# Diagonal sums by VectorE from scaled tiles in the later half of a fused linear-attention and MLP kernel, with a new order table

## The chip, the cores and the metric

The kernel runs on one core of one Trainium2 chip. The metric is device time in microseconds (us) of one execution, from launch to end; lower is better. The profile of one execution gives a span, from the first to the last recorded instruction, which is a little shorter than that execution's device time.

In the profile PE is TensorE's matrix multiply, PEld its weight load, DVE is VectorE, ACT is ScalarE, POOL is GpSimd and SP is SyncE, which here only starts transfers. A q behind an engine's name is its instruction queue.

## The reference

A linear attention with a decaying state feeds an MLP (all inputs float32, output 3072 x 384 float32):

```python
B, H, S, D = 4, 8, 768, 48
for t in range(S):
    cur = einsum('bhd,bhe->bhde', u * k[:, :, t], v[:, :, t])
    y[:, :, t] = einsum('bhd,bhde->bhe', r[:, :, t], state + cur)
    state = w * state + einsum('bhd,bhe->bhde', k[:, :, t], v[:, :, t])
x = y.transpose(0, 2, 1, 3).reshape(B * S, H * D)          # 3072 x 384
h = maximum(x @ w_in, 0)                                    # d_ff = 2048
out = (h * h) @ w_out
```

The term with `u` is the diagonal: at time t it adds `v[t] * sum_d(r[t,d] * u[d] * k[t,d])` for each head. These sums over d, eight per row (one per head), are what the change moves.

## The kernel before

The 768 time steps of each of the 4 batches are cut into 6 chunks of 128. A unit is one chunk of one batch: unit i has chunk i // 4 and batch i % 4, so there are 24. Units 0 to 5 are handled singly; units 6 to 23 in pairs (i, i + 1), where loads, transposes and some elementwise steps take both units at once, and the first matrix product of the MLP takes both as 256 columns.

Steps of a unit, by the names that the order table uses:

- `rt`, `kt`, `vt`: loads of r, k and v. SP's queue issues r and k (units 0 to 5 in two halves each, `rt.1.0` and `rt.1.1`), POOL's queue issues v of units 0 to 5; later v comes by SP too (`vtS` and `vt`). `ktA` is a load from ACT's queue.
- `scale.i.0` and `scale.i.1` (VectorE, L301 and L303): r times a rising and k times a falling power of w, into the bf16 tile `rkw`, 48 values of a head padded to 64.
- `turn`, `rkT` (TensorE, ScalarE; units 0 to 5) or `rkD` (one transposing DMA for a pair): `rkT`, r and k with head dimension on the partitions.
- `rk` (VectorE, L357 for pairs, L360 for single units): product of the transposed r and k, 128 x 1024 in bf16 for a pair.
- `at` (TensorE, L369): scores of a unit or pair; `mask` (VectorE, L377), two per unit: scores times the triangle.
- `d` or the first part of `s`: the diagonal sums, four products with `rk` as weights and `uwb` (u times w on a block diagonal) as 8 moving columns, L389 or L410. The second part of `s`, L398, is the state's update, left out for the last chunk. `sadd`, `sdec` (VectorE, L424, L428) and `stb` (ScalarE, L432) carry the state on.
- `dv` (VectorE, L420): v times the diagonal sums. `y` (TensorE, L441, L447): masked scores times v plus r times state. `yb` (VectorE, L456): their sum, bf16.
- `xturn`, `xT` or `xD` (a transposing DMA for a pair, L467): y transposed. `m1.i.s` (TensorE, L493): x times a quarter or an eighth of `w_in`; for a single unit, `m1.i.s` uses the weights `w_in_q` number s. `relu` (ScalarE, L501), `sqA` or `sqD` (square by ScalarE, L508, or by VectorE, L510). `m2` (TensorE, L517, and L533 for the last unit): times `w_out`. `osb` and `out`: the result's copy and its store.
- `I.q` and `O.q`: POOL's loads of the weights `w_in_q` and `w_out_q` number q. `ids`, `upper`, `zeros`, `copied`, `uwb`: small constants. `fill.n`: n products of a constant tile that give TensorE something to do.

The order table ORDER is a list of these words. The kernel walks it once and issues the instructions of each step as it meets the word; each engine and each queue then runs its own instructions in that order, and the number behind @ names the PSUM bank. A wait therefore holds everything that stands later on the same engine. The schedule is entirely this table. `by_rows`, `rows_of` and the like do not exist before.

Of the kernel before, what the change touches and what calls it, by code (L numbers as in the profile page):

```python
# [16 lines left out]
kt.0.0 kt.0.1 rt.0.0 rt.1.0 I.0 rt.1.1 vt.0 ktA.1.0 lnat.0 fill.26 log@4567 kt.1.1 lnat.1 ids rt.2.0 w.1 upper w.0  # L17
fill.8 cols@1 rt.2.1 wk scale.0.0 kt.2.0 zeros scale.0.1 wr fill.8 turn.0.0@2 kt.2.1 copied uwb turn.0.1@5 rkT.0.0
rt.3.0 rkT.0.1 vt.1 rk.0 fill.10 at.0@63 scale.1.0 rt.3.1 I.3 kb.0@4 mask.0.0 d.0@2 turn.1.0@7 I.2 kbT.0 kt.3.0
mask.0.1 rkT.1.0 vt.2 scale.1.1 vb.0 I.1 kt.3.1 fill.19 turn.1.1@4 dv.0 y.0@3 rkT.1.1 rt.4.0 yb.0 vb.1 rk.1 fill.9  # L20
kb.1@4 kt.4.0 scale.2.0 at.1@31 xturn.0@6 rt.4.1 mask.1.1 d.1@5 turn.2.0@2 xT.0 rkT.2.0 scale.2.1 kt.4.1 fill.5
m1.0.0@7 kbT.1 mask.1.0 turn.2.1@2 relu.0.0 dv.1 rt.5.0 fill.2 y.1@1 rkT.2.1 m1.0.3@4 yb.1 end rt.5.1 s.1@5
scale.3.0 relu.0.3 wend xturn.1@7 rk.2 at.2@26 xT.1 kb.2@0 mask.2.1 sqA.0.0 kt.5.0 d.2@4 turn.3.0@3 vt.3 s.0@7
sadd.1 rkT.3.0 m1.0.2@1 kt.5.1 scale.3.1 kbT.2 O.0 m1.1.0@6 mask.2.0 vb.2 relu.0.2 vt.4 turn.3.1@3 dv.2 m1.1.3@5
rt.6 rkT.3.1 sadd.0 O.1 y.2@1 relu.1.0 kt.6 m1.1.2@0 yb.2 relu.1.3 vt.5 at.3@72 rk.3 relu.1.2 kb.3@4 mask.3.1
xturn.2@6 sqA.1.0 O.2 m1.0.1@5 scale.4.0 xT.2 s.2@0 O.3 sqD.0.3 d.3@2 relu.0.1 m1.1.1@1 vb.3 mask.3.0 turn.4.0@3
kbT.3 m1.2.0@6 scale.4.1 relu.1.1 dv.3 m1.2.1@4 rkT.4.0 sqD.1.3 sqA.0.2 y.3@7 m1.2.2@1 scale.5.0 relu.2.1 sqD.1.1
m1.2.3@2 relu.2.2 sqD.0.1 s.3@5 sqA.1.2 turn.4.1@4 m2.0.0@3 sadd.3 relu.2.3 sadd.2 m2.1.0@1 rkT.4.1 yb.3 relu.2.0
m2.1.1 rk.4 vb.4 scale.5.1 kb.4@7 stb.1 xturn.3@6 at.4@42 kbT.4 m2.0.1 mask.4.1 xT.3 stb.0 s.4@5 mask.4.0 turn.5.0@6
m1.3.0@2 sqD.2.1 rkT.5.0 y.4@0 dv.4 relu.3.0 turn.5.1@6 rt.8 sadd.4 m1.3.3@7 rkT.5.1 yb.4 m2.1.2 sqA.3.0 sqA.2.0  # L30
m2.0.2 kt.8 xturn.4@2 m2.0.3 xT.4 scale.6.0 kb.5@5 osb.0 m2.1.3 scale.7.0 relu.3.3 m1.3.1@2 vtS.6 kbT.5 vb.5
m1.4.0@6 scale.6.1 scale.7.1 at.5@75 relu.4.0 m2.2.0@0 mask.5.0 osb.1 rkD.6 sqA.4.0 m1.4.1@4 sqD.2.3 sqA.2.2 sqD.3.3
m1.4.2@1 relu.3.1 mask.5.1 m2.2.1 stb.3 sdec.4 m1.4.3@6 relu.4.2 rt.10 rk.5 y.5@5 sqA.4.2 scale.8.0 s.5@2 scale.8.1
relu.4.1 m2.2.2 scale.9.0 relu.4.3 vtS.8 m1.3.2@1 sqD.3.1 stb.4 m2.3.0@4 dv.5 relu.3.2 yb.5 m2.2.3 scale.9.1 kt.10
m2.3.1 osb.2 sadd.5 sqA.4.1 m2.4.0@1 sqD.4.3 vb.6 xturn.5@0 sdec.5 at.6@2376 xT.5 rk.6 rkD.8 m2.4.1 stb.2 mask.7.0
stb.5 m1.5.0@0 sqA.3.2 mask.6.0 s.7@7 relu.5.0 mask.7.1 m1.5.3@5 mask.6.1 s.6@2 relu.5.3 m2.4.2 dv.6 out.0 vb.8
y.6@3 dv.7 rt.12 y.7@0 yb.6 m1.5.1@6 yb.7 m2.3.2 sadd.6 relu.5.1 xD.6 scale.10.0 m2.4.3 sqA.5.0 scale.10.1 sqA.5.1
m2.3.3 sadd.7 vtS.10 osb.4 m1.5.2@6 scale.11.1 scale.11.0 m2.5.0@3 relu.5.2 sqD.5.3 kt.12 m2.5.1 sqA.5.2 rk.8
at.8@1520 osb.3 sdec.6 m2.5.2 mask.9.0 rkD.10 m2.5.3 mask.8.0 s.8@4 mask.8.1 osb.5 s.9@2 m1.6.0@7 mask.9.1 m1.6.1@6
sadd.8 relu.6.0 dv.9 kt.14 m1.6.3@5 relu.6.1 dv.8 m1.6.7@1 sqA.6.0 scale.12.0 sadd.9 sqA.6.1 y.9@3 rt.14 y.8@4 vb.10  # L40
m1.6.2@0 yb.8 stb.6 m1.6.5@2 yb.9 relu.6.3 sdec.9 xD.8 m1.6.4@6 relu.6.5 scale.12.1 m2.7.0@3 relu.6.2 sqD.6.3
relu.6.7 vtS.12 m2.6.0@4 scale.13.0 relu.6.4 scale.13.1 m1.6.6@7 sqA.6.2 rk.10 at.10@6120 sqA.6.4 rkD.12 m2.6.1
relu.6.6 mask.10.0 sqA.6.5 s.10@5 sdec.7 m2.7.1 sqA.6.6 sqD.6.7 m2.7.2 stb.7 mask.10.1 stb.9 out.1 m2.7.3 sadd.10
kt.16 mask.11.0 y.10@6 osb.7 m1.8.0@1 dv.10 m1.8.1@2 rt.16 scale.14.0 relu.8.0 sdec.8 m1.8.3@5 relu.8.1 mask.11.1
m2.6.2 stb.8 yb.10 sqA.8.1 s.11@3 y.11@2 relu.8.3 dv.11 m1.8.6@1 vb.12 yb.11 m1.8.4@6 relu.8.6 sadd.11 xD.10 m2.6.3
rk.12 sqA.8.0 relu.8.4 scale.15.0 m1.8.2@2 scale.14.1 m1.8.5@0 relu.8.2 sdec.10 out.4 m2.9.0@7 osb.6 scale.15.1
vtS.14 sqA.8.2 sqD.8.3 m2.8.0@6 relu.8.5 out.3 at.12@4312 sqA.8.6 rkD.14 s.12@0 sqA.8.5 mask.13.0 m2.8.1 sqA.8.4
mask.12.1 m1.8.7@5 mask.12.0 m1.10.1@1 relu.8.7 mask.13.1 out.2 m1.10.3@3 relu.10.1 scale.16.0 vtS.16 s.13@4 sadd.12
# [35 lines left out]
def kernel(  # L84
# [130 lines left out]
    def fill():  # L215
        nc.tensor.matmul(out=banks[0][:, :128], lhsT=warm, rhs=warm, start=True, stop=True)  # L216
# [165 lines left out]
    def apart(i):  # L382
        return f" d.{i}@" in ORDER.replace("\n", " ")
# [239 lines left out]
```

## Time and profile before

| what | value |
|---|---|
| device time, median of 3 runs (lowest to highest) | 171.85 us (170.75 to 172.5) |
| device time of the profiled execution | 171.94 us |
| its span | 170.2 us |
| mean granted TensorE clock | 0.988 |
| DVE, ACT busy | 122.3 us, 129.8 us |

The profiled execution lies 0.09 us above the median of the runs, and 1.74 us of its device time lie outside the span. The busy time of PE is that of pipelined instructions, whose recorded durations overlap: how fast PE works is read from the distance between the starts of successive groups.

### The profile page before, as it was taken

The numbers are of one execution on the slowest core, as the hardware profiler recorded it, in microseconds if no ns is written. First come the engines' busy times: TensorE is split into PE (matmuls) and PEld (weight loads), VectorE is DVE, ScalarE is ACT, GpSimd is POOL, SyncE is SP. The second block draws the span as 40 slices with busy tenths as digits, with TensorE's granted clock in tenths as the row PEclk, the third lists the DMA queues.
The fourth block names the chain that finished last, engine by engine and source line by source line (L and its number), as shares of the span: only waits on it lengthen the run. The fifth ranks groups of instructions, "written<-read, shape, count | busy, mean of one in ns | idle before, by whom it ended". The sixth has DMA issues, their size and how long they took to land.

```text
span 170.2 us, 4733 instructions
## 1 busy us (share of the span) xinstructions
PE 163.9 (96%) x1947; PEld 134.1 (79%) x1947; DVE 122.3 (72%) x243; ACT 129.8 (76%) x255; POOL 15.7 (9%) x36
## 2 busy tenths in 40 slices
PE   7959999999999999999999999999999999999993
PEld 7649999778787697886977887787889789688672
DVE  6567999876999989988988888989697662101100
ACT  3735999888796489698499679688699739599921
POOL 7770670000000000000000000000000000000000
PEclk9996999999999999999999999999999999999999
DMA  3999999999999899999999997998990501100044
GB/s 92 172 279 240 272 194 254 213 201 227 185 181 218 153 214 190 181 212 191 236 182 202 174 251 173 188 288 197 180 232 4 179 6 54 42 0 4 0 164 162
DMA packets 91493, 28.86 MB, mean 170 GB/s; under 512 B 82864, under 2 KB 90672, under 8 KB 91472
## 3 DMA queue, kind: packets, MB, share of 16 engines
q1 hardware_dynamic: 88416, 23.99, 67.5%
q0 software_dynamic: 2624, 4.33, 12.9%
q8 instruction: 15, 0.25, 0.6%
q10 hardware_dynamic: 432, 0.25, 0.6%
q14 instruction: 6, 0.05, 0.1%
HBM read 20.50 MB, written 4.72 MB: 148 GB/s over the span
## 4 chain that ended last, share of the span: by engine, by line
PE 87%; DMA 6%; DVE 3%; SPq 2%; issue 1%; DVEq 0%
PE bank L493 36%; PE bank L517 34%; DMA rt<-in_r_dram 4%; PE bank L369 4%; PE bank L441 3%; DMA xT<-yb 2%; PE bank L398 2%; PE bank L447 2%; SPq L281 2%; PE bank L533 2%; PE bank L333 1%; PE bank L410 1%; PE bank L345 1%; PE bank L216 1%; PE bank L477 1%
## 5 line engine op out<-in xcount | busy, mean ns | idle before, releaser
L493 PE MATMUL bank<-xT,w_in_q 128*128 128x256 bf16 (+1 forms) x720 | 72.6, 251 | 0.1
L501 ACT ACTIVATE gr<-bank 128x512 f32<-128x512 f32 x96 | 55.3, 604 | 19.0 <-PE bank L493 15.2
L517 PE MATMUL bank<-w_out_q,g 128*128 128x384 bf16 x368 | 68.6, 326 | 0.0
L493 PEld LDWEIGHTS <-w_in_q 128*128 128x128 bf16 x720 | 63.8, 113 | 3.9 <-DMA xT<-yb 0.3
L517 PEld LDWEIGHTS <-g 128*128 128x128 bf16 x368 | 34.3, 98 | 18.1 <-issue 0.2
L508 ACT ACTIVATE g<-gr 128x512 bf16<-128x512 f32 x68 | 41.2, 636 | 0.2
L377 DVE TENSOR_TENSOR am<-bank,smask 128x512 bf16<-128x512 f32 x48 | 31.3, 684 | 7.4 <-PE bank L369 6.6
L510 DVE TENSOR_TENSOR g<-gr 128x512 bf16<-128x512 f32 x28 | 19.0, 686 | 17.2 <-ACT gr L501 17.2
L524 ACT COPY osb<-bank 128x384 f32<-128x384 f32 x23 | 11.0, 480 | 5.7 <-PE bank L517 5.6
L456 DVE TENSOR_TENSOR yb<-bank,dv 128x384 bf16<-128x384 f32 x24 | 12.9, 553 | 3.2 <-PE bank L447 2.3
L420 DVE TENSOR_TENSOR dv<-vb,bank 128x384 f32<-128x384 bf16 x24 | 13.0, 548 | 2.2 <-PE bank L410 1.4
L432 ACT CAST stb<-st 128x384 bf16<-128x384 f32 x20 | 10.2, 522 | 0.6 <-DVE st L428 0.6
L301 DVE TENSOR_TENSOR rkw<-rt,wpos 128x384 bf16<-128x384 f32 x18 | 9.8, 551 | 0.8 <-DMA rt<-in_r_dram 0.7
L301 DVE TENSOR_TENSOR rkw<-kt,wneg 128x384 bf16<-128x384 f32 x18 | 9.7, 551 | 0.8 <-DMA kt<-in_k_dram 0.8
L337 ACT COPY rkT<-bank 128x512 bf16<-128x512 bf16 x12 | 7.0, 590 | 3.4 <-PE bank L333 3.4
L216 PE MATMUL bank<-warm 128*128 128x128 bf16 x87 | 8.4, 265 | 1.1 <-DVE warm L161 1.1
L441 PE MATMUL bank<-vb,am 128*128 128x48 bf16 x192 | 8.9, 185 | 0.0
L428 DVE TENSOR_TENSOR st<-st,wend 128x384 f32<-128x384 f32 x16 | 8.8, 550 | 0.0
L424 DVE TENSOR_TENSOR st<-bank,st 128x384 f32<-128x384 f32 x16 | 8.7, 549 | 0.0
L441 PEld LDWEIGHTS <-am 128*128 128x128 bf16 x192 | 7.9, 97 | 0.8
L369 PE MATMUL bank<-rkT 64*128 64x128 bf16 x192 | 8.2, 221 | 0.2 <-ACT rkT L337 0.2
L216 PEld LDWEIGHTS <-warm 128*128 128x128 bf16 x87 | 7.0, 121 | 1.2 <-DVE warm L161 1.0
(75 smaller groups left out, 120.8 us busy)
## 6 DMA issues: line engine op xcount, KB each, us to landing
out_dram<-osb SPq DMA_DIRECT2D x23, 192.0 KB, 2.4
rt<-in_r_dram SPq DMA_DIRECT2D x9, 384.0 KB, 5.8
kt<-in_k_dram SPq DMA_DIRECT2D x9, 384.0 KB, 5.2
vt<-in_v_dram SPq DMA_DIRECT2D x9, 384.0 KB, 4.5
w_in_q<-in_moe_w_in_dram POOLq DMA_DIRECT2D x4, 384.0 KB, 8.3
w_out_q<-in_moe_w_out_dram POOLq DMA_DIRECT2D x4, 384.0 KB, 8.8
vt<-in_v_dram POOLq DMA_DIRECT2D x6, 192.0 KB, 7.3
kt<-in_k_dram SPq DMA_DIRECT2D x11, 96.0 KB, 5.2
```

The costliest lines, as they stand in the source:

```text
L216: nc.tensor.matmul(out=banks[0][:, :128], lhsT=warm, rhs=warm, start=True, stop=True)
L301: nc.vector.tensor_tensor(t["rkw"][:, x, :, :, :D], pair(src), pair(wneg if x else wpos), ALU.mult)
L369: nc.tensor.matmul(out=t["at"][o][:, p, :], lhsT=t["rkT"][sl, 1, p, :], rhs=t["rkT"][sl, 0, p, :], start=True, stop=True,)
L377: nc.vector.tensor_tensor(am, t["at"][o], smask.unsqueeze(1).to_broadcast([C, HP, C]), ALU.mult)
L420: nc.vector.tensor_tensor(t["dv"], t["vb"], t["d"].unsqueeze(2).to_broadcast([C, H, D]), ALU.mult)
L441: nc.tensor.matmul(out=y[:, 2 * p + o, :], lhsT=t[f"am{o}"][:, p, :], rhs=t["vb"][:, 2 * p + o, :], start=(o == 0 and p == 0), stop=c == 0 ...
L456: nc.vector.tensor_tensor(t["yb"], t["y"], t["dv"].rearrange("p h d -> p (h d)"), ALU.add)
L493: nc.tensor.matmul(out=t["h", s][:, a], lhsT=turned, rhs=chunks[c]["xT"][:, b : b + m, n, :], start=(n == 0), stop=(n == NK - 1),)
L501: nc.scalar.activation(t["gr", s], t["h", s], AF.Relu)
L508: nc.scalar.activation(g, x, AF.Square)
L510: nc.vector.tensor_tensor(g, x, x, ALU.mult)
L517: nc.tensor.matmul(out=t["o"], lhsT=chunks[units[i][0]]["g"][:, f, units[i][1], :], rhs=w_out_q[f // 4][:, f % 4, :], start=(f == 0), stop ...
```

## The change

For pairs 12 to 22 (units 12 to 23) the sums no longer go through the transposed tiles. VectorE makes three instructions of a pair instead of the one `rk`: `dx` multiplies the scaled r and k of both units (128 x 768, bf16 in and out, into the buffers of `rk`), `du` multiplies this by a row of u times w that lies on every partition (128 x 768, bf16 and float32 in, float32 out, into the tile of `dv`), and `dr` adds up the 48 values of each head (128 x 768 to 128 x 16). `dv` reads these sums from SBUF instead of PSUM. TensorE's four products with 8 columns go away for these 12 units; `s.20` to `s.23`, which held nothing else, go away altogether. Units 0 to 11 keep the old way.

The row of u times w needs two more loads on POOL's queue, `wB` and `uB` (each one row of 384 values to all 128 partitions, into buffers of `osb`), and one product on POOL, `uw`. The loads of w and u that the columns need (`wu`) and the logarithm `lnw` become words of the table. `dv` becomes a tile of a pair with 2 buffers. Four squares move from VectorE to ScalarE (28 to 24 `sqD`, 68 to 72 `sqA`); `rk` goes from 15 to 9. The table is another one from its first line on.

```diff
+    def spread_row(name):
+        rows[name] = mpool.tile([128, dm], F32, name="osb")
+        src = dict(uB=u, wB=w)[name].rearrange("h d -> (h d)")
+        nc.gpsimd.dma_start(out=rows[name], in_=src.unsqueeze(0).to_broadcast([128, dm]))
+
+    def uw_row():
+        nc.gpsimd.tensor_tensor(uw, rows["uB"], rows["wB"], ALU.mult)
...
+    def by_rows(i):
+        return i >= NH and f" dx.{i // 2 * 2} " in ORDER.replace("\n", " ")
+
+    def rows_of(i):
+        whole = two("rk", i, work, [128, HP, C], bufs=RKB)
+        return whole.rearrange("p u a c -> p u (a c)")[:, :, :dm]
+
+    def diag_product(i):
+        x = rkw_b[i // 2 % NPAD].rearrange("p u x a o e -> p u x (a o) e")[:, :, :, :, :D]
+        nc.vector.tensor_tensor(rows_of(i).rearrange("p u (h d) -> p u h d", h=H), x[:, :, 0], x[:, :, 1], ALU.mult)
+
+    def diag_weigh(i):
+        whole = of_two("dv", i, work, [C, H, D], F32, bufs=2)
+        nc.vector.tensor_tensor(
+            whole.rearrange("p u h d -> p u (h d)"), rows_of(i), uw.unsqueeze(1).to_broadcast([128, 2, dm]), ALU.mult
+        )
+
+    def diag_add(i):
+        whole = of_two("dd", i, work, [C, H], F32, bufs=3)
+        nc.vector.tensor_reduce(whole, two("dv", i, work, [C, H, D], F32, 2), axis=mybir.AxisListType.X, op=ALU.add)
...
     def sums(i):
         c, b = units[i]
         whole = bank("s", i)
-        if not apart(i):
+        if not apart(i) and not by_rows(i):
...
     def diag_v(i):
         t = tiles[i]
-        t["dv"] = work.tile([C, H, D], F32, name="dv")
-        nc.vector.tensor_tensor(t["dv"], t["vb"], t["d"].unsqueeze(2).to_broadcast([C, H, D]), ALU.mult)
+        of_two("dv", i, work, [C, H, D], F32, bufs=2)
+        d = t["dd"] if by_rows(i) else t["d"]
+        nc.vector.tensor_tensor(t["dv"], t["vb"], d.unsqueeze(2).to_broadcast([C, H, D]), ALU.mult)
...
-kt.0.0 kt.0.1 rt.0.0 rt.1.0 I.0 rt.1.1 vt.0 ktA.1.0 lnat.0 fill.26 log@4567 kt.1.1 lnat.1 ids rt.2.0 w.1 upper w.0
+wu kt.0.0 rt.0.0 kt.0.1 rt.1.0 wB lnw rt.1.1 vt.0 ktA.1.0 lnat.0 fill.26 log@4567 kt.1.1 lnat.1 w.0 ids rt.2.0 w.1
...
```

At the start of the program, POOL's instructions before, from its constants on (`vt` is v of unit 1, then of unit 2; `w_in_q0` was issued well ahead of this, just behind the loads of w and u):

```order
L226 MEMSET uwb_136 128x32
L227 MEMSET wend_146 128x384
L256 TENSOR_TENSOR cols_126<-cols_126 128x4
L259 CAST uwb_136<-cols_126 64x4 x2
L311 DMA vt_162<-in_v_dram 128x8x48
L288 DMA w_in_q3_150<-in_moe_w_in_dram 128x3x512
L288 DMA w_in_q2_149<-in_moe_w_in_dram 128x3x512
L311 DMA vt_310<-in_v_dram 128x8x48
L288 DMA w_in_q1_148<-in_moe_w_in_dram 128x3x512
```

The same place on POOL now:

```order
L302 DMA w_in_q0_142<-in_moe_w_in_dram 128x3x512
masks.py:65 MEMSET smask_130 128x128
masks.py:66 AFFINE_SELECT smask_130<-smask_130 128x128
L232 MEMSET uwb_131 128x32
L233 MEMSET wend_141 128x384
L262 TENSOR_TENSOR cols_121<-cols_121 128x4
L265 CAST uwb_131<-cols_121 64x4 x2
L325 DMA vt_232<-in_v_dram 128x8x48
L302 DMA w_in_q3_145<-in_moe_w_in_dram 128x3x512
L302 DMA w_in_q2_144<-in_moe_w_in_dram 128x3x512
L302 DMA w_in_q1_143<-in_moe_w_in_dram 128x3x512
```

`w_in_q0` has moved behind the loads of w's row and of v of units 0, 1 and 2, and between the product for `uwb` and `w_in_q3` stands the load of v of unit 3 instead of that of unit 1.

On VectorE, from the first scaling (of unit 0) on, before (`cols` is the copy that POOL's product for `uwb` waits for, L253):

```order
L303 TENSOR_TENSOR rkw0_127<-rt_88,wfour_123 128x8x48
L303 TENSOR_TENSOR rkw0_127<-kt_155,wfour_123 128x8x48
L253 COPY cols_126<-bank1_77 128x8
L360 TENSOR_TENSOR rk_267<-rkT_241 128x512
L303 TENSOR_TENSOR rkw0_127<-rt_88,wfour_123 128x8x48
L377 TENSOR_TENSOR am0_294<-bank6_257,smask_135 128x512
L377 TENSOR_TENSOR am1_307<-bank3_79,smask_135 128x512
L303 TENSOR_TENSOR rkw0_127<-kt_155,wfour_123 128x8x48
L420 TENSOR_TENSOR dv_340<-vb_313,bank2_78 128x384
L456 TENSOR_TENSOR yb_353<-bank3_79,dv_340 128x384
```

And now:

```order
L317 TENSOR_TENSOR rkw0_122<-rt_88,wfour_118 128x8x48
L317 TENSOR_TENSOR rkw0_122<-kt_154,wfour_118 128x8x48
L259 COPY cols_121<-bank6_252 128x8
L374 TENSOR_TENSOR rk_279<-rkT_227 128x512
L412 TENSOR_TENSOR am1_306<-bank6_252,smask_130 128x512
L412 TENSOR_TENSOR am0_309<-bank2_78,smask_130 128x512
L374 TENSOR_TENSOR rk_279<-rkT_227 128x512
L456 TENSOR_TENSOR dv_340<-vb_293,bank3_79 128x384
L317 TENSOR_TENSOR rkw1_123<-rt_208,wfour_118 128x8x48
L492 TENSOR_TENSOR yb_359<-bank7_253,dv_340 128x384
L412 TENSOR_TENSOR am0_376<-bank2_78,smask_130 128x512
```

Both scalings of unit 1 (the two rows at the top of this fence; unit 0's stand just ahead of them) now come ahead of the copy of the columns and of unit 0's masks.

In the later half, on VectorE around the masks of a pair, before (pair 14: `rk`, four masks, then `dv` and `yb` of both units, with the state and squares between):

```order
L357 TENSOR_TENSOR rk_1845<-rkT_1667 128x1024
L377 TENSOR_TENSOR am1_1852<-bank2_78,smask_135 128x512
L377 TENSOR_TENSOR am0_1860<-bank5_256,smask_135 128x512
L377 TENSOR_TENSOR am1_1872<-bank6_257,smask_135 128x512
L377 TENSOR_TENSOR am0_1875<-bank4_255,smask_135 128x512
L420 TENSOR_TENSOR dv_1899<-vb_1854,bank0_76 128x384
L456 TENSOR_TENSOR yb_1931<-bank4_255,dv_1899 128x384
```

And now for the same pair, the last row being the `dx` of pair 16:

```order
L412 TENSOR_TENSOR am0_1847<-bank4_250,smask_130 128x512
L412 TENSOR_TENSOR am1_1856<-bank5_251,smask_130 128x512
L389 TENSOR_TENSOR dv_1864<-rk_1759,lnat_117 128x768
L412 TENSOR_TENSOR am1_1874<-bank0_76,smask_130 128x512
L395 TENSOR_REDUCE dd_1883<-dv_1864 128x16
L456 TENSOR_TENSOR dv_1864<-vb_1788,dd_1883 128x384
L412 TENSOR_TENSOR am0_1905<-bank2_78,smask_130 128x512
L456 TENSOR_TENSOR dv_1864<-vb_1788,dd_1883 128x384
L385 TENSOR_TENSOR rk_1933<-rkw0_122 128x2x384
```

`du` and `dr` stand between the masks; `dx` stands one pair ahead.

More of the change, by code (lines that the diff above doesn't have):

```diff
@@ L22 @@
[L22 to L36, printed above, removed]
@@ L80 @@
+out.18 m2.22.2 osb.23.0 out.19 m2.22.3 out.17 m2.23.1@3 out.23.0 osb.22 out.22 osb.23.1 out.23.1
 """
```

139 lines of the change are left out of this document (79 added, 60 removed).

## The prediction

> **What bounds the kernel now.** I read the page, then the busy time by stage, then the chain of work that ended last, and last the engines' rows in time at the places that the change touches.
>
> ```profile
> span 170.2 us, 4733 instructions
> ...
> PE 87%; DMA 6%; DVE 3%; SPq 2%; issue 1%; DVEq 0%
> ...
> 16.37:78.20 61.83, 61.83 (x864) 51.24 (x862) 56.83 (x110) 52.96 (x108) 5.82 (x9) 1.00 1.02 205
> 78.20:138.20 60.00, 59.94 (x689) 48.69 (x689) 50.12 (x94) 47.52 (x91) 0.00 (x0) 1.00 0.93 187
> 138.20:167.70 29.50, 29.12 (x240) 23.09 (x238) 5.15 (x9) 21.68 (x43) 0.00 (x0) 1.00 0.16 53
> ...
> 166.43 0.91 PE bank L533 x16
> ```
>
> The stage rows give start and end, length, and then busy us of PE, PEld, DVE, ACT and POOL (with counts), the granted clock and the DMA share. From 16.4 us, where the first product of the MLP starts, to 167.3 us TensorE has no hole worth the name, at full clock. Before that it waits for loads and fills. So the time is a start of 16.4 us, 151 us of TensorE work and an end of some 3 us, and a change gains only by taking work from TensorE or by an earlier start. VectorE is busy for 50.1 of 60 us in the stage where the change works, so it has 9.9 us to give there. The execution took 171.94 us, 1.74 us more than its span and 0.09 us more than the median 171.85; the sum is made against 171.94.
>
> **What TensorE loses: the 8-column products.**
>
> ```profile
> 90.84 0.24 PE L410 MATMUL bank<-uwb,rk 128*128 128x8 bf16 x4
> 90.94 0.33 PE L398 MATMUL bank<-vb,rkw 128*128 128x96 bf16 x4
> 91.11 0.25 PE L410 MATMUL bank<-uwb,rk 128*128 128x8 bf16 x4
> 91.21 0.33 PE L398 MATMUL bank<-vb,rkw 128*128 128x96 bf16 x4
> ...
> 137.94 0.25 PE L410 MATMUL bank<-uwb,rk 128*128 128x8 bf16 x4
> 138.05 1.48 PE L493 MATMUL bank<-xT,w_in_q 128*128 128x256 bf16 x12
> ...
> L410 PEld LDWEIGHTS <-rk 128*128 128x128 bf16 x80 | 4.5, 97 | 1.3
> ...
> 78.20:138.20 60.00, 2.96 (x48) 2.75 (x48) 1.00 0.93 187
> ```
>
> The last row is of L410 alone: 48 products, units 12 to 23, stand in the stage. Their recorded 2.96 us overlap with their neighbours. What a group costs is the distance from its start to the next group's: 0.10 us (90.84 to 90.94, 91.11 to 91.21), 0.11 us (137.94 to 138.05). Twelve groups give 12 x 0.105 = 1.27 us, all on the path: term one, -1.27 us. It is 0.7% of the time, so even a perfect trade is less than the 1% that a measurement of this kernel can tell from no change.
>
> The Trainium skill, page "TensorE: Matmul & The Clock Gate", section "LDWEIGHTS (loading the stationary operand)", says that a weight load takes its columns / 1.2 ns, 107 ns for 128. If each of the 48 loads were paid so, 5.1 us would go, an estimate from that page. The row's own 97 ns is near it, but four pairs of load and product start within 0.10 us, so the trace bears out overlap, and the sum doesn't use it.
>
> **What VectorE gains and loses.**
>
> ```profile
> 99.25 0.55 DVE L301 TENSOR_TENSOR rkw<-rt,wpos 128x384 bf16<-128x384 f32 x1
> 99.72 0.55 DVE L424 TENSOR_TENSOR st<-bank,st 128x384 f32<-128x384 f32 x1
> ...
> 102.58 0.68 DVE L357 TENSOR_TENSOR rk<-rkT 128x1024 bf16<-128x1024 bf16 x1
> 103.19 0.55 DVE L301 TENSOR_TENSOR rkw<-kt,wneg 128x384 bf16<-128x384 f32 x1
> 103.66 0.68 DVE L377 TENSOR_TENSOR am<-bank,smask 128x512 bf16<-128x512 f32 x1
> 104.26 0.55 DVE L428 TENSOR_TENSOR st<-st,wend 128x384 f32<-128x384 f32 x1
> ...
> DVE am L377 <- PE bank L369: 3.1, 3, 1.4
> DVE yb L456 <- PE bank L447: 1.8, 3, 1.2
> ...
> DVE am L377 <- ACT g L508: 0.7, 1, 0.7
> ```
>
> From start to start, back to back, 384 float32 take 0.47 us, 512 take 0.60 us, and the 1024 bf16 of `rk` 0.61 us. So 128 more float32 cost 0.13 us, and 768 would take 0.47 + 3 x 0.13 = 0.87 us. `du` has a float32 operand: 0.87 us. `dr` has no row; at the rate of `rk` it would be 0.47 us, at that of float32 0.87 us; it reads float32, so 0.87. `dx` is bf16 like `rk` but with runs of 48: between 0.47 and 0.87 us, and I take 0.47, since `rk` is the nearest in type. A pair then costs 2.21 us more and 0.61 less; six pairs 9.6 us; the four squares that leave (0.60 each) take back 2.4: +7.2 us against 9.9 free, or +9.6 with a slow `dx`.
>
> The Trainium skill, page "VectorE: DVE Perf Modes", section "The perf-mode tier table (the rule you actually need)", gives reductions one element a cycle and bf16 two-tensor work two. By that rule `dx` is 0.47 and `dr` 0.87, as taken; no run here shows either yet.
>
> That leaves 2.7 us of slack in the stage, while the trace shows 5.6 us of waits there that end with TensorE or ScalarE (3.1 + 1.8 + 0.7). If all of them stayed, the stage would be 2.9 us late. But most of such a wait is VectorE being early: a later VectorE finds the scores done. I take +0.5 us, nearer to the lower end; the bounds are 0 and +2.9, with a slow `dx` +5.3. The waits of `dv` on L410 end, but their cover is the same TensorE.
>
> ScalarE takes the four squares in its 12.5 free us of the stage: nothing. `uw` and the row loads run on POOL, which has nothing after 25 us but `vt.5`, now queued behind them:
>
> ```profile
> 22.46 0.92 POOL L311 DMA_DIRECT2D vt<-in_v_dram x1
> ...
> L318 ACT CAST vb<-vt x6: 500/523/547, 11.7 to 38.2; 128x384 bf16<-128x384 f32 x6
> ```
>
> It was issued 16 us before its cast at 38.2; that cover shrinks, as `uw` must first see `uB` land. I put 0 here, between 0 and +1.
>
> The transposing DMAs on SP's queue stand elsewhere too:
>
> ```profile
> xT<-yb SPq DMA_TRANSPOSE x9, 3.1
> ...
> 80.64 1.24 PEld L493 LDWEIGHTS <-w_in_q 128*128 128x128 bf16 x12 [0.32 <-DMA xT<-yb]
> ```
>
> One of the nine was waited for, 0.3 us. In the new table at least eight groups of MLP products of 0.65 us, or as much other work, stand between each `xD` and the pair's first `m1`, 5 us for a transpose of 3.1: nothing, between 0 and +1.
>
> **The start.** What is late next is here.
>
> ```profile
> 10.13 0.56 DVE L303 TENSOR_TENSOR rkw<-rt,wfour 128x384 bf16<-128x384 f32 x1 [1.63 <-DMA rt<-in_r_dram]
> 10.60 1.28 DVE L377 TENSOR_TENSOR am<-bank,smask 128x512 bf16<-128x512 f32 x2
> 11.80 0.55 DVE L303 TENSOR_TENSOR rkw<-kt,wfour 128x384 bf16<-128x384 f32 x1
> ...
> 4.32 0.60 SPq L281 DMA_DIRECT2D kt<-in_k_dram x1
> ...
> kt<-in_k_dram SPq DMA_DIRECT2D x1, 96.0 KB, 7.1
> ...
> 6.82 0.15 DVE L253 COPY cols<-bank 128x8 f32<-128x8 f32 x1
> ...
> 8.58 1.52 POOL L288 DMA_DIRECT2D w_in_q<-in_moe_w_in_dram x2
> ...
> DMA to landing us min/median/max: 7.0/8.3/11.0
> ...
> 16.26 0.83 PE L493 MATMUL bank<-xT,w_in_q 128*128 128x128 bf16 x12
> 17.47 0.84 PE L493 MATMUL bank<-xT,w_in_q 128*128 128x128 bf16 x12
> ...
> q0 software_dynamic: 2624, 4.33, 12.9%
> ```
>
> The second half of k of unit 1 (issued at 4.32, landing 7.1 us on) lands at 11.4. POOL's transfers took 12.9% of 170.2 us for 4.33 MB, so the 0.38 MB of `w_in_q0` are some 2 us of all DMA engines; the row of w that takes their place is half of it. I put the landing, K, at 10.4 (9.4 to 11.4). Now this half's scaling stands ahead of the copy of the columns and of unit 0's masks. From K: scaling 0.47 and the copy give 0.75 us; from the end of a copy (6.97) to the issue of `w_in_q3` (8.58) were 1.6 us with one load of v between, as now; the four weight loads took 7.0 us at least. `w_in_q3` is there at K + 9.4 = 19.8 us. The chain on VectorE (scaling, copy, `rk`, two masks, `rk`, `dv`, scaling, `yb`, mask, scaling, mask, by the distances above 5.7 us, and `y.1` of unit 1) lets `m1.0.0` start at K + 6.1 = 16.5. Behind it stand 1.8 us of other work, then `m1.0.3`, which needs `w_in_q3`: TensorE, in order, waits from 18.3 to 19.8. Some 0.7 us of work (`s.0`, `s.1`, `y.1`, two fills) has moved ahead of `m1.0.0`, so with equal work left `m1.0.3` would stand at 18.9 us on the old clock (16.37, plus the 1.8 us and the 0.7 us). Term three: 19.8 - 18.9 = +0.9 us. Its ends: -1.6 if K is 9.4 and the weights are never late (9.4 + 6.1 + 1.8 = 17.3), and +5.9 with K 11.4 and a landing of 11.0 (24.8).
>
> **The sum:** 171.94 - 1.27 + 0.5 + 0.9 = 172.1 us.
>
> **The rivals.**
> The start is on time (chance 0.21). `w_in_q0` out of the way speeds up every early load, and `w_in_q3` comes by 18.3. Then `m1.0.3` stands at 17.3 to 18.3 instead of 18.9, and with VectorE covered the time is 171.94 - 1.27 - 0.6 to 1.6 = 169.1 to 170.1, say 169.6. For it: the first scaling of unit 1 waited 1.63 us for a load. Against it: 7.0 us is the shortest of four landings.
>
> The weights land at the median or worse (0.20). 8.3 instead of 7.0 adds 1.3, 11.0 adds 4.0: 173.4 to 176.1, say 174. It decides from a landing of `w_in_q3` after 21 us. For it: POOL now issues one load more ahead. Against it: `w_in_q0` no longer shares the early transfers.
>
> VectorE becomes the bound in pairs 12 to 20 (0.19). One mechanism: `dx` at 0.87 us leaves 0.3 us in the stage, and waits on scores push masks and `y` late; from 2.7 to 5.3 us: 171.94 - 1.27 + 0.9 + 2.7 to 5.3 = 174.3 to 176.9, say 174.5. It decides where VectorE shows no idle time and TensorE waits for masks at `y`. For it: 50.1 of 60 us busy already. Against it: bf16 at double rate in `rk`.
>
> The products cost TensorE their full weight loads (0.04): with 48 x 0.097 us from the row of the loads the time is 171.94 - 4.66 + 1.4 = 168.7. The starts 0.10 us apart speak against it. The rule of the Trainium skill's page on TensorE, above, would have it so.
>
> **How the numbers follow.** My forecast, 171.0 to 173.2, has 0.36. Faster by over 1% is below 170.13, slower above 173.57. Faster: 0.21 + 0.04 = 0.25. Slower: 0.17 of the late weights and 0.16 of VectorE, 0.33. Within 1%: the forecast and what is left of these two, 0.42. The range is 169.4 to 175.0; outside it lie the 0.04, some 0.03 of the early start, 0.05 and 0.08 of the two slow rivals' ends.
>
> **What would show it.** Right: no L410-like product after unit 11 and 12 groups of 0.1 us fewer; `du` and `dr` near 0.95 us recorded, `dx` near 0.55; TensorE idle for 1 to 2 us ahead of the second group of MLP products, released by the load of `w_in_q`; a hole of under 1 us in all on TensorE between 80 and 140 us. Wrong: no such hole at the start, or holes over 2 us at `y` with VectorE full, or a `vb` of unit 5 that waits for its load.

## The result and the profile after

| | before | after |
|---|---|---|
| device time, median of 20 runs (lowest to highest) | 171.09 us (170.3 to 172.5) | 172.49 us (171.52 to 173.99) |
| ratio, 95% interval | | 1.0076 [1.0052, 1.0099] |
| device time and span of the profiled execution | 171.94, 170.2 us | 172.98, 171.1 us |
| mean granted clock of that execution | 0.988 | 0.989 |

The changed kernel is slower by 0.76%, inside the 1% that the prediction called no change; 172.1 us was forecast. The terms behind that number came out less well than the number. All ratios leave out executions that were over 1.5% slower than the fastest of the same kernel: one of e10 (174.35 us), one of e12 (331.73 us) and one of the kernel before. First the page of the changed kernel and its stages (columns as before: PE, PEld, DVE, ACT, POOL, clock, DMA):

```profile
span 171.1 us, 4670 instructions
...
PE 80%; DMA 15%; SPq 2%; DVE 1%; issue 1%; ACT 0%; DVEq 0%
...
16.44:78.90 62.46, 61.04 (x851) 50.24 (x847) 57.20 (x110) 50.47 (x101) 4.62 (x8) 1.00 1.05 204
78.90:139.30 60.40, 59.50 (x641) 47.86 (x641) 56.67 (x102) 50.24 (x98) 0.00 (x0) 1.00 0.92 178
139.30:168.30 29.00, 28.84 (x249) 23.03 (x245) 3.90 (x8) 21.50 (x43) 0.00 (x0) 1.00 0.20 67
```

TensorE, full in both long stages before (61.83 of 61.83 and 59.94 of 60.00), now misses 1.42 and 0.90 us there, and DMA's share of the chain that ended last went from 6 to 15%. VectorE went from 50.12 to 56.67 us in the second stage. The new instructions of VectorE, by form:

```profile
L389 DVE TENSOR_TENSOR dv<-rk,lnat 128x768 f32<-128x768 bf16 x6 | 5.7, 949 | 0.0
L395 DVE TENSOR_REDUCE dd<-dv 128x16 f32<-128x768 f32 x6 | 5.7, 943 | 0.0
L385 DVE TENSOR_TENSOR rk<-rkw 128x768 bf16<-128x768 bf16 x6 | 3.3, 548 | 0.0
```

`du` 949, `dr` 943 and `dx` 548 ns: the sizes forecast (0.95, 0.95 and 0.55 recorded). Then TensorE's rows in time: the two first products of the MLP, and the three scores of a pair that waited in the middle.

```profile
16.48 0.84 PE L529 MATMUL bank<-xT,w_in_q 128*128 128x128 bf16 x12
...
18.49 0.40 PE L404 MATMUL bank<-rkT 64*128 64x128 bf16 x8 [0.44 <-ACT rkT L351]
...
19.67 0.83 PE L529 MATMUL bank<-xT,w_in_q 128*128 128x128 bf16 x12 [0.46 <-DVE am L412]
...
67.17 0.62 PE L404 MATMUL bank<-rkT 64*128 64x128 bf16 x16 [0.53 <-DMA rkT<-rkw]
...
89.50 0.62 PE L404 MATMUL bank<-rkT 64*128 64x128 bf16 x16 [0.30 <-DMA rkT<-rkw]
...
101.73 0.62 PE L404 MATMUL bank<-rkT 64*128 64x128 bf16 x16 [0.60 <-DMA rkT<-rkw]
```

These waits are the time that TensorE misses: 0.44 + 0.46 + 0.53 us in the first long stage, 0.30 + 0.60 us in the second. `m1.0.3` starts at 19.67 us (19.8 forecast), but what released it is a mask: `m1.0.3@6` uses the PSUM bank that the second half of `at.2@26` holds until `mask.2.1` has read it (two masks from 18.93 us on, 0.69 us each: 19.62). The weights came 0.4 us sooner. First VectorE's and POOL's rows in time, then the landing of the weights issued at 11.39 us (number, KB, us to landing):

```profile
18.93 1.29 DVE L412 TENSOR_TENSOR am<-bank,smask 128x512 bf16<-128x512 f32 x2
...
11.39 2.26 POOL L302 DMA_DIRECT2D w_in_q<-in_moe_w_in_dram  x3
...
34.70 1.01 POOL L282 TENSOR_TENSOR lnat<-osb 128x384 f32<-128x384 f32 x1 [14.67 <-DMA osb<-in_u_dram]
35.65 0.96 POOL L325 DMA_DIRECT2D vt<-in_v_dram  x1
```

```profile
w_in_q<-in_moe_w_in_dram POOLq DMA_DIRECT2D x1, 384.0 KB, 7.8
```

The weights land at 19.2 us. POOL's last two rows are `uw`, which waited 14.67 us for the row of u and held its queue for that time, and the load `vt.5` behind it; the cast of that v was not waited for by TensorE, so that term was 0 as taken.

From these two executions: -1.27 us of products, +0.77 at the start (19.67 instead of the neutral 18.9), +1.43 for the three transposes: +0.93 us, against +0.9 of span. The 18.9 is the prediction's own estimate of where `m1.0.3` would stand with nothing late. Counted back from TensorE's end (148.46 us from 19.67 on, less the 1.43 of waits, plus 1.27 of products, ahead of the 167.32 us at which TensorE ends before) it is 19.0, so the start is 0.65 to 0.77. This accounts for one pair of executions. The experiments test whether it holds for others.

### The profile page after: what moved, and what is told of

Same layout as the page of the kernel before. It is cut to its first block, busy times and chain, and to the rows that moved or that the text cites. A ratio compares the mean times of both kernels' runs of the same rounds, so it can differ in the third digit from the quotient of the medians.

```text
span 171.1 us, 4670 instructions
## 1 busy us (share of the span) xinstructions
PE 163.2 (95%) x1899; PEld 133.4 (78%) x1899; DVE 129.4 (76%) x251; ACT 131.3 (77%) x259; POOL 17.9 (10%) x39
## 3 DMA queue, kind: packets, MB, share of 16 engines
q1 hardware_dynamic: 88416, 23.99, 68.5%
## 4 chain that ended last, share of the span: by engine, by line
PE 80%; DMA 15%; SPq 2%; DVE 1%; issue 1%; ACT 0%; DVEq 0%
PE bank L553 32%; PE bank L529 31%; DMA rkT<-rkw 12%; PE bank L404 4%; DMA rt<-in_r_dram 3%; PE bank L477 2%; PE bank L213 2%; PE bank L433 2%; SPq L295 2%; PE bank L569 2%; PE bank L483 2%; PE bank L347 1%; PE bank L359 1%; PE bank L513 1%; DVE am L412 0%
## 5 line engine op out<-in xcount | busy, mean ns | idle before, releaser
L553 PE MATMUL bank<-w_out_q,g 128*128 128x384 bf16 x368 | 67.5, 326 | 0.0
L537 ACT ACTIVATE gr<-bank 128x512 f32<-128x512 f32 x96 | 54.2, 602 | 17.2 <-PE bank L529 15.6
L544 ACT ACTIVATE g<-gr 128x512 bf16<-128x512 f32 x72 | 43.6, 637 | 0.2
L546 DVE TENSOR_TENSOR g<-gr 128x512 bf16<-128x512 f32 x24 | 16.2, 683 | 12.8 <-ACT gr L537 12.7
L213 PE MATMUL bank<-warm 128*128 128x128 bf16 x87 | 9.2, 278 | 1.1 <-DVE warm L161 1.1
L404 PEld LDWEIGHTS <-rkT 64*128 64x128 bf16 x192 | 5.5, 95 | 5.5 <-DMA rkT<-rkw 2.8
L213 PEld LDWEIGHTS <-warm 128*128 128x128 bf16 x87 | 7.6, 128 | 1.3 <-DVE warm L161 1.0
```

Of the source, the lines that this page charges most:

```text
L404: nc.tensor.matmul(out=t["at"][o][:, p, :], lhsT=t["rkT"][sl, 1, p, :], rhs=t["rkT"][sl, 0, p, :], start=True, stop=True,)
L537: nc.scalar.activation(t["gr", s], t["h", s], AF.Relu)
L544: nc.scalar.activation(g, x, AF.Square)
L546: nc.vector.tensor_tensor(g, x, x, ALU.mult)
L553: nc.tensor.matmul(out=t["o"], lhsT=chunks[units[i][0]]["g"][:, f, units[i][1], :], rhs=w_out_q[f // 4][:, f % 4, :], start=(f == 0), stop ...
```

## The experiments

Each kernel was timed in five rounds beside the kernel before on the same chip (no run is called e3 or e4); the ratio is to that kernel, whose median was 170.61 us beside the first four, 170.93 beside the next four and 170.60 beside the last four.

| kernel | median us | ratio, 95% interval |
|---|---|---|
| e1, two-unit transposes issued earlier | 173.22 | 1.0146 [1.0110, 1.0181] |
| e2, other PSUM bank | 171.83 | 1.0084 [1.0053, 1.0114] |
| e5, before without the 48 products, new 32-byte tile | 172.30 | 1.0106 [1.0075, 1.0137] |
| e6, after without VectorE's sums, new 32-byte tile | 173.60 | 1.0177 [1.0143, 1.0210] |
| e7, after again | 172.04 | 1.0072 [1.0035, 1.0108] |
| e8, before again | 170.89 | 0.9987 [0.9960, 1.0015] |
| e9, as e5 without the tile | 170.95 | 0.9996 [0.9969, 1.0023] |
| e10, as e6 without the tile | 172.05 | 1.0069 [1.0038, 1.0101] |
| e11, the sums by VectorE in the old table | 176.16 | 1.0305 [1.0261, 1.0350] |
| e12, earlier weights and other bank | 171.73 | 1.0044 [1.0013, 1.0076] |
| e13, before with an unused 32-byte tile | 172.10 | 1.0061 [1.0031, 1.0091] |
| e14, before, rkw on 64-byte bounds | 170.92 | 1.0012 [0.9982, 1.0041] |

**The two waits that the profile showed, one at a time (e1, e2).** The edits are words of the table: in e1 `rkD.10`, `rkD.14` and `rkD.16` move ahead in SP's queue, in e2

```diff
-m1.0.3@6
+m1.0.3@0
```

> The new kernel with three words of the table moved: the transposing DMAs of pairs 10, 14 and 16 go ahead of the stores and loads that stood before them on SP's queue. In the new kernel's profile TensorE stood idle for 0.53, 0.30 and 0.60 us before the scores of these pairs, released by those transposes. Theory (late transposes cost the time): those 1.4 us go, so about 171.1 us against 172.5, equal to the kernel before within 0.5 us. Rival (VectorE is what limits that stage): the idle time reappears at the masks or at y, and the time stays within 0.4 us of 172.5.

> The new kernel with one PSUM bank number changed: the second group of MLP products (m1.0.3) writes bank 0 instead of bank 6, which the masks of unit 2 still read. Theory (bank): m1.0.3 starts at about 19.2 us instead of 19.67, when its weights have landed, and 0.4 us go: about 172.1. Rival, the prediction's own account (only the load of w_in_q3 holds it): it starts at 19.67 as before and nothing changes.

In e1 the scores of the pairs no longer wait, and still the kernel is not faster than the changed one (1.0146 against 1.0076). In e2, where the transposes stand as in the changed kernel, they were not waited for either. So those waits come and go with the execution: of the six profiles with the new table that leave `rkD` where it is, two show them (1.43 us, and 0.34 us in e12) and four none of 0.2 us. Why e1 lost more stays open; some 0.4 us of it lie outside the span, as its six executions are 2.1 to 2.3 us longer than their spans and those of the changed kernel 1.7 to 1.9 us. For the start the two kernels' rows are, e1 first:

```profile
16.08 0.84 PE L528 MATMUL bank<-xT,w_in_q 128*128 128x128 bf16 x12
19.28 0.86 PE L528 MATMUL bank<-xT,w_in_q 128*128 128x128 bf16 x12 [0.47 <-DMA w_in_q<-in_moe_w_in_dram]
```

```profile
16.37 0.84 PE L528 MATMUL bank<-xT,w_in_q 128*128 128x128 bf16 x12
18.98 0.86 PE L528 MATMUL bank<-xT,w_in_q 128*128 128x128 bf16 x12
```

With another bank the product starts at 18.98 without a wait, and only the `y` behind it waits 0.32 us for its mask; with the old bank and a slightly earlier start it waits for the weights. The mask and the weights are two gates a few tenths of a microsecond apart, and taking one away moves the start to the other: the group of products behind that `y` starts 4.00 us after the first product in e2 (16.37 to 20.37) and 4.06 us after it in the changed kernel (16.48 to 20.54), and the ratio of e2, 1.0084, is no better than 1.0076. A third wait, 0.4 us ahead of the scores of unit 2 for ScalarE's copy of `rkT`, stands in all seven profiles with the new table, and no experiment touches it.

**The sums, one side at a time (e5, e6, then e9, e10).** In e5 the kernel before loses its 48 products, in e6 the changed kernel loses `dx`, `du` and `dr`. In all four the diagonal sums of units 12 to 23 are left out and `dv` multiplies by a stand-in: in e5 and e6 a new tile of 32 bytes per partition filled with zeros,

```diff
+    dzero = const.tile([128, H], F32)
...
+        nc.gpsimd.memset(dzero, 0.0)
```

in e9 and e10 eight columns of the mask that is there already (`smask[:, :H]`).

> The kernel before without the 48 products with 8 columns of units 12 to 23; dv reads a constant tile, so the diagonal term of these units is left out, and all else is as before. Theory (0.105 us a group, all on the path): 1.27 us less than the kernel before, 169.8 against 171.1. Rival (each weight load is paid in full, 0.097 us): 4.7 us less, 166.4. Rival (the groups fill time that is lost anyway): no change.

> The new kernel without its 18 new VectorE instructions (dx, du, dr); dv reads a constant tile, so the diagonal term of units 12 to 23 is left out. Theory (VectorE's 2.2 us a pair lie beside TensorE): at most 0.4 us less than 172.5, and the waits for the transposes of pairs 10, 14 and 16 stay. Rival (VectorE is the bound in pairs 12 to 20): 1.5 to 3 us less.

Both took work away and became slower, by 1% against what they were cut from. Both expectations fell, and the new suspect was the tile: it moves every later tile of SBUF by 32 bytes. Hence e9 and e10, with the two controls e7 and e8:

> The changed kernel as it is, beside the kernel before on one chip, as a control for the others of this group. If the difference belongs to the kernel and not to the chip, the ratio is 1.005 to 1.010 again; if it belonged to the chip or to single executions, it is 1.000 within 0.003. In its profile the waits of TensorE for the transposing DMA of rkT (1.43 us in three places in the first profile, none in the run with the other bank) come back by theory (rkD issued too late in the queue), and are under 0.3 us by the rival (they come and go with the execution).

> The kernel before against itself: ratio 1.000 within 0.003, which says how far two kernels must stand apart here. Its profile is the one on the same chip as the others': packets of the first queue at 67.5% of the span as in the first profile (theory that the layout of SBUF sets that share); anything from 67 to 72% if the share belongs to the execution.

> The kernel before without the 48 eight-column products of units 12 to 23, and dv reads eight columns of the mask that is there already instead of a new 32-byte tile (the diagonal sums of those units are left out, the weight is a stand-in). Theory, that the new tile made the earlier version slow by moving every later tile of SBUF by 32 bytes: the packets of the first queue go back from 72.0% to 67 to 69% of the span, and the products' 12 x 0.105 = 1.27 us come off: 0.990 to 0.996. Rival, that the products were a cover for transfers that end last without them: 1.008 to 1.013 again, with waits for xT<-yb of 0.5 us and more.

> The changed kernel without the three VectorE instructions on each pair (dx, du, dr), dv reading eight columns of the mask that is there already (the diagonal sums of units 12 to 23 are left out). Theory, that the new 32-byte tile made the earlier version slow: 74.4% of the first queue goes back to 68 to 70%, and the ratio to that of the changed kernel, 1.004 to 1.010, less at most 0.002 for VectorE, whose 14.6 us of sums lay beside TensorE's work. Rival, that the three sums' absence reorders the transfers: 1.014 to 1.021 again.

The difference belongs to the kernel: the changed one has 1.0072 in these rounds too, and the kernel before against itself 0.9987. Without the tile, e10 stands at 1.0069, as the changed kernel: no cost of VectorE's 14.7 us of sums is seen in the new table, though intervals of 0.5 to 0.6 us to each side could hide a small one. The profile of e7, which has the sums, agrees: TensorE is busy for all of the 120 us from 40 to 160. e9 stands at 0.9996, not at the forecast 0.990 to 0.996: the products that went out of TensorE do not show in the time. Its profile says where they went. Rows in time of e8, then of e9: the same group of twelve products of the start, the last products, and the last stores of SP.

```profile
19.73 0.83 PE L493 MATMUL bank<-xT,w_in_q 128*128 128x128 bf16 x12
...
164.91 1.06 PE L533 MATMUL bank<-w_out_q,g 128*128 128x128 bf16 x16
...
161.92 2.31 SPq L553 DMA_DIRECT2D out_dram<-osb  x5
...
166.32 0.33 SPq L549 DMA_DIRECT2D out_dram<-osb  x1
```

```profile
20.37 0.83 PE L495 MATMUL bank<-xT,w_in_q 128*128 128x128 bf16 x12
...
164.12 1.06 PE L535 MATMUL bank<-w_out_q,g 128*128 128x128 bf16 x16
...
161.13 3.86 SPq L555 DMA_DIRECT2D out_dram<-osb  x5
...
162.52 1.99 SPq L555 DMA_DIRECT2D out_dram<-osb  x1
```

Queue q8 loads blocks of instructions. Its last row (packets, MB, share of 16 engines) in e8 from 156 to 158 us, then in e9 from 162 to 163 us:

```profile
q8 instruction: 1, 0.02, 3.8%
```

```profile
q8 instruction: 1, 0.02, 11.7%
```

From the same group to TensorE's end are 146.24 us in e8 (19.73 to 165.97) and 144.81 in e9 (20.37 to 165.18): 1.43 us less, so term one is real. But the end behind TensorE grows from 2.83 us (168.8 - 165.97) to 4.12 (169.3 - 165.18), by 1.29 us: one store took 1.99 us to issue where five took 2.31 together, and the three after it follow late. Of the 1.29 us some 0.56 are the later issue of the last store (0.91 us behind TensorE's end instead of 0.35), the rest its longer way from there to the end of the span. In the microsecond of the slow store a block of instructions was loaded. In the kernel before this load falls some 10 us ahead of TensorE's end, into a stretch without stores. The group at the start stands 0.64 us later in e9, which makes up the spans: +0.64 - 1.43 + 1.29 = +0.5. The edit does not touch the start, so the first of these terms is the execution's.

The coincidence holds over all fourteen profiles of the case. Four (before, e8, e13, e14) have the load at 156 to 158 us, no store among the last eight that takes over 0.45 us to issue, and an end of 2.82 to 2.88 us. Ten (all that lost the products; e5, e9 and e11 with the old table) have it in the last 2 to 4 us of TensorE's work, a store of 0.86 to 2.35 us, and an end of 2.97 to 4.12 us, 3.49 on the mean: +0.64 us. TensorE has 3,894 products and weight loads before and 3,798 after, far more than any other engine, and the queue loads 0.25 MB in 15 blocks, so the blocks are presumably TensorE's; with 96 instructions fewer (48 products and their weight loads), the same number of instructions is reached nearer to the end. That the load lies there is shown; that it is what delays the store was not tried by itself. The Trainium skill, page "Runtime: NRT & Kernel Launch", section "Instruction fetch mechanics", says that an engine's instructions are refilled in blocks of 16 KiB by a DMA queue of its own and that crossing such a bound is mostly hidden. The size agrees (0.25 MB in 15). That it is hidden from the engine agrees too: in e8 and e9 no wait of TensorE over 0.2 us stands behind 20 us. For the stores of another queue beside it the coincidence above speaks against it.

**The start at full clock (e7 against e8, e12).** In both first profiles TensorE's clock fell for some 4 us in the start, in e7 and e8 it did not. Stages of TensorE in the first profile before, then in that after (start and end, length, busy us with the count, granted clock, DMA share, GB/s):

```profile
12.00:14.00 2.00, 1.80 (x25) 0.60 1.14 205
14.00:16.00 2.00, 2.00 (x28) 0.55 1.18 233
```

```profile
10.00:12.00 2.00, 1.98 (x28) 0.61 1.03 205
12.00:14.00 2.00, 2.00 (x32) 0.54 1.18 293
```

Rows of e8 and then e7:

```profile
18.13 1.53 PE L493 MATMUL bank<-xT,w_in_q 128*128 128x128 bf16 x24 [0.26 <-DMA w_in_q<-in_moe_w_in_dram]
```

```profile
15.25 0.84 PE L529 MATMUL bank<-xT,w_in_q 128*128 128x128 bf16 x12
...
18.79 0.86 PE L529 MATMUL bank<-xT,w_in_q 128*128 128x128 bf16 x12 [0.81 <-DMA w_in_q<-in_moe_w_in_dram]
...
19.69 0.84 PE L529 MATMUL bank<-xT,w_in_q 128*128 128x128 bf16 x12
...
165.14 1.06 PE L569 MATMUL bank<-w_out_q,g 128*128 128x128 bf16 x16
```

From 19.69 us TensorE has 146.51 us to go in e7 (to 166.20), from 19.73 it has 146.24 in e8, although e7 has 1.27 us less of products: it has done 1.54 us less work by then. The start is what is left over in this sum: start +1.5, products -1.3, end +0.4 (3.20 instead of 2.83): +0.6, the 168.8 and 169.4 us of span. But e7's execution is a short one of its kind. e10, whose start is that of the changed kernel word for word, has a span of 170.3 us at full clock, near the median of the changed kernel there (170.4). Its row of `m1.0.3`:

```profile
19.22 0.86 PE L529 MATMUL bank<-xT,w_in_q 128*128 128x128 bf16 x12 [1.24 <-DMA w_in_q<-in_moe_w_in_dram]
```

By the same sum (20.12 us to TensorE's end at 166.58 are 146.46 us) it has start +1.9, products -1.3, end +0.9 (3.72 instead of 2.83): +1.5, the 168.8 and 170.3 us. So a start that waits for the weights and a longer end account for the loss at full clock, less the products.

In e7 the first product starts 1.2 us earlier than in the first profile, and the weights let it through 0.9 us earlier only. So e12 moves the load of `w_in_q3` right behind that of `w_in_q0` and takes the other bank:

```diff
-kt.2.1 I.0 fill.2 cols@6
+kt.2.1 I.0 I.3 fill.2 cols@6
...
-I.3 kb.1@5 scale.2.0
+kb.1@5 scale.2.0
...
-m1.0.3@6
+m1.0.3@0
```

> The changed kernel with two words of its start altered: the last quarter of the first weights is issued right behind the first one, not behind two value loads, and the product m1.0.3 goes to PSUM bank 0 instead of bank 6. Theory, that the start costs the time: m1.0.3 begins at 17.9 to 18.3 us instead of 18.8 to 19.7, without a wait for w_in_q or a mask, and the ratio comes down from 1.0072 to 1.000 to 1.004. Rival, that the time lies in the rest of the table (transfers in the middle, the stores of the tail): it stays at 1.006 to 1.010 although m1.0.3 is earlier.

Its rows:

```profile
15.87 0.84 PE L528 MATMUL bank<-xT,w_in_q 128*128 128x128 bf16 x12
...
18.44 0.83 PE L528 MATMUL bank<-xT,w_in_q 128*128 128x128 bf16 x12
19.66 0.37 PE L476 MATMUL bank<-vb,am 128*128 128x48 bf16 x8 [0.39 <-DVE am L411]
```

`m1.0.3` itself has no wait; 18.44 us is 0.14 later than expected, 2.57 behind the first product instead of 3.19 and 3.54. But the `y` behind it waits 0.39 us for its mask, as in e2, so that part of the gain is lost again. The ratio is 1.0044, of which the interval overlaps that of the changed kernel: it points to the theory, and the medians alone do not settle it. Executions of one kind of clock (the clock held or fell, see the base below) point the same way: on this chip e12 loses 0.4 us of span where the clock held (three executions, 169.1 against 168.7) and 0.05 where it fell (eight, 169.95 against 169.9), so much of its 1.0044 goes with the clock, which fell in 8 of its 11 executions and in 4 of 29 of the kernel before.

**The sums in the old table (e11).** The code of the changed kernel, with the words of the table before; in place of each `rk` of pairs 12 to 22 stands `dx`, and behind the next masks `du` and `dr`.

> One part of the change alone: the sums of units 12 to 23 by VectorE, in the order table of before (dx stands where rk stood, du and dr one mask step further on; the two loads for the row of u times w behind the last weight load). Theory, that the new table's start costs the time and the sums cost nothing: the start is that of before, and the ratio is 0.990 to 1.000 (the 12 x 0.105 = 1.27 us of products are gone from TensorE, of which the run without them showed 0.1 us in the median). Rival, that VectorE's three instructions on each pair delay what it owes TensorE: 1.004 and above, with idle time of TensorE behind VectorE between 80 and 140 us.

The rival won, by far. TensorE's waits between 75 and 140 us (us in total, times, longest), then VectorE's rows at one pair:

```profile
PE bank L477 <- DVE am L412: 1.9, 4, 0.9
PE bank L529 <- DVE yb L492: 1.0, 1, 1.0
PE bank L433 <- DVE am L412: 0.8, 2, 0.6
```

```profile
89.13 0.69 DVE L412 TENSOR_TENSOR am<-bank,smask 128x512 bf16<-128x512 f32 x1
89.74 0.95 DVE L389 TENSOR_TENSOR dv<-rk,lnat 128x768 f32<-128x768 bf16 x1
90.61 0.68 DVE L412 TENSOR_TENSOR am<-bank,smask 128x512 bf16<-128x512 f32 x1
91.21 0.94 DVE L395 TENSOR_REDUCE dd<-dv 128x16 f32<-128x768 f32 x1
```

With 0.3 us behind a square these waits come to 4.0 us, most of the 5.1 us by which the span is longer than that of e8. Between the masks for which TensorE waits stand 0.95 us of `du` and of `dr`. VectorE's share is no higher than in the changed kernel (56.4 of 60 us from 80 to 140, against 56.67 of 60.40), but there the new work stands where no one waits for what is behind it, and four squares have left. The sums are free with the new table, not by themselves; what the order does and what the four squares do was not tried apart.

**The shift by 32 bytes (e13, e14).** Unused tiles in the kernel before, nothing else:

```diff
     uwb = const.tile([128, HP, H], BF16)
+    pad = const.tile([128, 8], F32)
```

> The kernel before with one unused tile of 32 bytes in each partition behind uwb: the same instructions in the same order, every later tile of SBUF 32 bytes further on, so that loads, transposes and stores work on rows that begin at 32 modulo 64 bytes. Theory, that this shift made the two runs with the constant tile slow: 1.008 to 1.013, with the packets of the first queue at 71 to 74% of the span instead of 66.9%. Rival, that the extra fill by GpSimd at the start or the data did it: 1.000 within 0.003, and 67%.

> The kernel before with two unused tiles (32 bytes behind cols, 96 bytes behind wend_c), so that the scaled tiles rkw, the sources of the first transposes, begin at a multiple of 64 bytes instead of 32 modulo 64, and all tiles behind wend keep their remainder modulo 128. Theory, that the layout matters to whatever a transfer reads or writes: the transposes of rkw land 0.3 to 1 us earlier (6.0 us in the median before), the ratio is 0.996 to 1.000 since TensorE does not wait for them in the kernel before. Rival, that only the tiles written by loads matter: 6.0 us, and 1.000 within 0.003.

Queue q1 of e8 and of e13, with the transposes of the scaled tiles:

```profile
q1 hardware_dynamic: 88416, 23.99, 66.9%
...
rkT<-rkw SPq DMA_TRANSPOSE x9, 6.0
```

```profile
q1 hardware_dynamic: 88416, 23.99, 75.1%
...
rkT<-rkw SPq DMA_TRANSPOSE x9, 7.4
```

The same 88416 packets and 23.99 MB take 75.1 instead of 66.9% of the engines' time, the transposes land 1.4 us later, and TensorE waits 0.6 us for `xT<-yb`. The share is 72.0% in e5 and 74.4% in e6, and 65.9 to 69.5% in the eleven profiles without the shift; the later landing is seen in e5 (7.4 us) and not in e6 (6.2, where the changed kernel has 5.8 to 6.8). The tile slows the kernel by itself, by 0.6%, a little less than expected; the rest of the 1% in e5 and e6 stays open. e14 shows no effect of the place of `rkw` on the time, nor of moving all tiles behind `wend_c` by 128 bytes (1.0012), so a shift as such is not what costs. That it is the remainder modulo 64 is argued from the sizes of the tiles; the profile has no addresses. In the changed kernel itself the share is 68.5 and 69.2% (first profile and e7, against 67.5 and 66.9 before), so this is an effect of e5 and e6, not a part of the change.

No kernel here is measurably faster than the kernel before.

## Why the prediction was right in the time and wrong in its steps

- **Term one, -1.27 us.** Right where it was priced: 1.43 us from the same group to TensorE's end in e9 against e8. What failed is that all of it counted as time: the instruction load moved into the last stores, which the prediction had priced at nothing, and goes with an end that takes back 0.64 us on the mean of the profiles, 1.29 in e9. By the mean e9 should have gained 0.8 us; its interval allows 0.5, so 0.64 is rather too little for it.
- **VectorE, +0.5 us.** The three durations were right. The term came out as 0 (e10 against e7, and TensorE without a hole from 40 to 160 us in e7), its lower end, as far as medians with some 0.5 us of interval to each side tell. That VectorE becomes bound was a fair rival: it is what happens in the old table (e11, 1.0305), with idle TensorE at masks as described. The new table avoids it.
- **The start, +0.9 us.** The step was right in place and close in time (16.5 and 19.8 forecast, 16.48 and 19.67 measured, +0.77), and the closeness is luck. K, the landing of the second half of k, was put at 10.4 us (9.4 at the earliest), but its scaling starts at 9.03 us in the first profile, 8.81 in e7 and 8.96 in e10; where the clock held the first product starts at 15.25 and 15.24 us (e7, e10), and it is 1.2 us later in the first profile, where the clock fell. The 7.0 us of landing were 7.8. The 1.8 us from the start of the first product to `m1.0.3` were 2.2 (e2: 18.98 - 16.37, less its wait of 0.44). Its cause was half right: the weights are one gate (e1, e7, e10), the bank shared with the scores of unit 2 the other (e2), and the prediction had not looked at the number behind @, nor at ScalarE's copy, which holds the scores for 0.44 us. So the sign that it named, 1 to 2 us of idle TensorE released by the load of `w_in_q`, is there in e10 (1.24 us) and not in the first profile. Its size was that of one kind of execution, as the next point shows.
- **The base.** The sum was made against an execution of 171.94 us with a granted clock of 0.988. Of 71 executions of the kernel before beside the experiments, 55 held the clock (mean at least 0.995) with a median span of 168.8 us, 16 did not, with 169.9. For the changed kernel (first result and e7) it is 9 of 29 with 170.4 and 20 with 170.55. The fall lasts some 4 us in the start (rows above). The kernel before loses by it what TensorE loses: the group of products that starts at 19.73 us in e8 starts at 21.20 in the first profile, 1.47 us later, and the span is 1.4 us longer. The changed kernel waits for loads there and loses less: `m1.0.3` starts at 18.79 and 19.22 us where the clock held (e7, e10), at 19.67 and 19.28 where it fell (the first profile, e1). So the loss is 0.65 us where the clock fell and 1.6 where it held, and the sum, taken from the former kind, could only show the smaller. These medians mix chips; in the rounds of e7 alone the two losses are 0.3 us (seven executions of the changed kernel) and 1.15 us (two), smaller and in the same order. The base was 0.85 us above the later median of 171.09; without that error the same sum had given 171.2 us, 1.3 too low. So that the number came within 0.4 us is luck: the forecast change was +0.1 us, the measured one +1.4.
- **The transposing DMAs, 0.** The prediction looked at `xD` ahead of `m1` and not at `rkD` ahead of the scores. In the profiled execution that was +1.43 us; in others 0 to 0.34. A miss, of a size that mostly does not occur.
- **`vt.5` behind `uw`, and the four squares, 0.** Right.

What is not settled: of the 1.6 us where the clock held, e7's accounting covers 0.6 (its execution is 1.0 us below the median of its kind) and that of e10 covers 1.5, in a kernel without the sums; no run repairs the whole start (in e12 the waits for the copy of `rkT`, 0.44 us, and for the mask, 0.39, are left) or moves the instruction load by itself; and why the clock falls in 20 of 29 executions with the new table and 16 of 71 with the old is open.

## What to carry to other kernels

Before a sum is made against one execution, see from the other runs which kind it is: a start that a fallen clock has already made late hides what a later load costs. Taking instructions from an engine seems to move where its instruction blocks are loaded, too; look whether the last one falls among the last stores, where a longer end went with it here. And an experiment that adds a tile, however small, shifts all tiles behind it, so that its stand-ins are best read from a tile that is there.

## What the hardware showed that was not expected

- Unused 32 bytes in each partition, with all later tiles 32 bytes on (e13): the same packets took 75.1 instead of 66.9% of the DMA engines' time, and the kernel 0.6% longer (1.0061 [1.0031, 1.0091]). The Trainium skill, page "DMA: Bandwidth & Descriptors", section "Constraints", asks for 32-byte alignment of a transpose in SBUF; a shift by 32 bytes keeps it, and the transposes still landed after 7.4 instead of 6.0 us.
- A load of one instruction block beside the last stores goes with a store that takes 1.99 us to issue in e9 (0.86 to 2.35 us over ten profiles), against at most 0.45 in the four without it. That the one causes the other was not tried.
